# The second query group of an attention-and-MoE kernel in tiles of 128, 64 and 128 rows, the tile of 64 shared by two heads

## The chip, the cores and the metric

The kernel runs on one core of one Trainium2 chip. The metric is the device time of one execution in microseconds; smaller is better. TensorE (PE) multiplies and transposes into the accumulator banks, VectorE (DVE), ScalarE (ACT) and GpSimd (POOL) work on elements, SyncE (SP) issues the transfers.

## What is computed

Four batches of 576 positions and eight heads of 64 go through causal attention with a bias from a running sum, then 2304 rows of width 512 through two gated layers of hidden width 1536. Cut to what matters:

```
scores = scale * np.matmul(q, k.transpose(0, 1, 3, 2))
cum = np.cumsum(np.maximum(s, 0.0), axis=-1)
bias = -(cum[:, :, :, None] - cum[:, :, None, :])
scores = np.where(causal, -1e9, scores + np.minimum(bias, 0.0))
attn = softmax(scores)
x = np.matmul(attn, v)               # then 2304 rows of 512
xn = x / rms(x) * rms_g
x = (silu(xn @ w_gate) * (xn @ w_val)) @ w_out
x = (silu(x @ w2_gate) * (x @ w2_val)) @ w2_out
```

## The kernel before

The program is not written in its final order. Each step is given to a planner (`Plan`, `op`) with its engine, an estimated cost, what it reads and writes, and a rank (`pri`). The planner goes through the steps in its own time and issues on each engine the ready step of the lowest rank. A step of PE that another engine released counts as ready 1500 ns later (`SLACK`), unless PE has nothing else; one that PE's own last step released counts as ready at once. The order so found is the program's, fixed per engine.

*Heads.* The queries of a head fall into group A (0 to 255) and group B (256 to 575). Tiles are in `QT`; B has tiles 2, 3 and 4 with 128, 128 and 64 rows. Batches 0 and 1 do group A in a short form at the start (`EarlyUnit`); everything else goes through `Head` and `Unit`, one head after the other (`attend`): 32 heads have a group B, 16 of them also a late group A. Operands are split into a high and a low part (`kHH`, `kLL`; `H`, `L`), so a product of two needs two matmuls for attention and three for the gated layers.

For one head and group B: `scores` (L624) multiplies each query tile with the keys up to its last row: 384 columns for tile 2, 512 for tile 3, twice 288 for tile 4, each for `kHH` and `kLL` (L636). POOL writes the mask of the diagonal block (L650), DVE adds bias and takes the least (L662), ACT takes the exponential (L673). `values` (L678) transposes twelve blocks of 128x128 on PE into banks `tp` (L700), five, five and two; ACT copies each bank to `pTB` high (L705), DVE subtracts for `pTB` low (L708); ten value products (L716) of 320, 320, 320, 192 and 64 columns, high and low, sum the head's output. `pTB` is one pair of buffers for all heads. ACT and DVE carry the result to `x`.

*Gated layer.* When all eight heads of a group are done, `normalise` scales its rows and `moe1` multiplies them with the first weights (L929, 24 matmuls of 256 or 320 columns for each of 12 rows). These MoE products rank behind all heads (`P_MOE`), so PE takes them whenever no step of a head is ready. Behind the heads come the rest of these products, then the first output product in a Strassen form (L1281), the second layer (L1451, L1527) and the last output product (L1281, L1336).

*Start.* `setup` clears buffers on DVE and POOL: in `clear` the pads of `sq` and `qst`, in `clear_scores` all of `sc4` outside its own rows (L536, L537), as a tile of 64 rows is transposed with 128.

## Time and profile before

| what | value |
|---|---|
| median of three runs | 1064.9 us (1063.16 to 1066.07) |
| the profiled execution | 1063.1 us, of which the traced span 1061.3 us |
| PE busy | 1045.8 us, 99% |
| DVE, ACT, POOL busy | 784.7, 640.6, 222.2 us |
| granted TensorE clock | 1.0 throughout, the level of 2.4 GHz |
| moved by DMA | 206.97 MB, mean 195 GB/s |

Busy time is the union of the instructions' rows. A matmul's row lasts until its result has drained, and the next starts inside it, so PE can be busy all the time and still have matmuls further apart than their columns ask for; the timeline's starts tell the distance. A window's row gives each engine's busy time in a stretch. The chain of waits follows the program back from its end.

### The profile page before, as it was taken

What the parts mean: (1) busy time and instruction counts of PE and PEld (TensorE: products, weight loads), DVE (VectorE), ACT (ScalarE), POOL (GpSimd) and SP (SyncE); (2) the same over time, 40 slices, a digit from 0 to 9 for tenths busy, and PEclk for the clock granted to TensorE, in tenths of its full rate; (3) what the DMA queues carried; (4) which work ended last, traced back from release to release, by engine and by line L of the source; (5) the groups of instructions that cost most, each with busy time, mean ns of one, the idle gap of its engine ahead of it and who ended that gap; (6) DMA issues with size and microseconds to landing.
All of it is one profiled execution on the core that took longest, in us unless ns stands there. A gap on an engine that the chain in (4) does not pass through costs nothing.

```text
span 1061.3 us, 19650 instructions
## 1 busy us (share of the span) xinstructions
PE 1045.8 (99%) x6436; PEld 946.4 (89%) x6436; DVE 784.7 (74%) x1945; ACT 640.6 (60%) x1371; POOL 222.2 (21%) x302
## 2 busy tenths in 40 slices
PE   7999999999999999999999999999999999999998
PEld 5699999999999999999987889888888888878888
DVE  7898887877788876657779888566568766876462
ACT  6898767767664664333466766554556544664552
POOL 3157434423322420000000000222113220300000
PEclk9999999999999999999999999999999999999999
DMA  6785454333436652657588672675757667878773
GB/s 194 245 301 162 121 137 134 109 98 112 130 105 229 233 160 57 204 176 233 189 283 267 195 234 62 224 231 191 252 193 254 232 224 272 283 252 264 216 237 107
DMA packets 124822, 206.97 MB, mean 195 GB/s; under 512 B 15600, under 2 KB 52464, under 8 KB 124720
## 3 DMA queue, kind: packets, MB, share of 16 engines
q1 hardware_dynamic: 124672, 205.65, 61.1%
q8 instruction: 51, 0.84, 0.3%
q14 instruction: 51, 0.42, 0.1%
q10 hardware_dynamic: 48, 0.07, 0.0%
HBM read 141.09 MB, written 64.56 MB: 194 GB/s over the span
## 4 chain that ended last, share of the span: by engine, by line
PE 86%; DVE 2%; DMA 2%; ACT 1%; issue 1%; ACTq 0%; DVEq 0%; SPq 0%
PE mo L929 23%; PE mo L1451 10%; PE sps L1451 8%; PE mo L1281 8%; PE tp L1281 6%; PE sps L1281 5%; PE tp L700 4%; PE tp L716 4%; PE sps L636 4%; PE mo L1527 3%; PE sps L929 2%; PE tp L929 2%; PE mo L1336 2%; PE tp L1451 1%; PE mo L836 1%; DMA hh<-row0T 1%
## 5 line engine op out<-in xcount | busy, mean ns | idle before, releaser
L929 PE MATMUL mo<-xH,H 128*128 128x256 f32 (+1 forms) x672 | 200.4, 299 | 0.1
L929 PE MATMUL mo<-xH,L 128*128 128x256 f32 (+1 forms) x672 | 199.2, 297 | 0.0
L929 PE MATMUL mo<-xL,H 128*128 128x256 f32 (+1 forms) x672 | 199.2, 296 | 0.0
L1177 DVE TENSOR_TENSOR hL<-hh,hH 128x512 fp32r<-128x512 f32 (+1 forms) x192 | 125.7, 667 | 69.9 <-ACT hH L1174 69.2
L1174 ACT ACTIVATE hH<-hh 128x512 fp32r<-128x512 f32 (+1 forms) x192 | 114.7, 602 | 93.9 <-DVE hL L1177 20.8
L673 ACT ACTIVATE sc<-sc,col 128x512 f32<-128x512 f32 (+4 forms) x160 | 96.0, 601 | 52.6 <-DVE col L662 51.8
L929 PEld LDWEIGHTS mo<-xH,H 128*128 128x128 f32 x672 | 126.2, 188 | 1.0 <-issue 0.3
L929 PEld LDWEIGHTS mo<-xL,H 128*128 128x128 f32 x672 | 126.2, 188 | 0.9 <-issue 0.2
L929 PEld LDWEIGHTS mo<-xH,L 128*128 128x128 f32 x672 | 126.2, 188 | 0.4
L1281 PE MATMUL mo<-hH,wo 128*128 128x512 f32 x312 | 97.7, 389 | 0.0
L1281 PEld LDWEIGHTS mo<-hH,wo 128*128 128x128 f32 x312 | 58.6, 188 | 12.3 <-ACT hH L1174 0.2
L700 PE MATMUL tp<-ident,sc 128*128 128x128 f32 x432 | 66.5, 276 | 0.0
L936 ACT ACTIVATE t<-mo 128x256 f32<-128x256 f32 (+1 forms) x84 | 34.0, 405 | 52.3 <-PE mo L929 52.0
L708 DVE TENSOR_TENSOR pTB<-tp,pTB 128x512 fp32r<-128x512 f32 (+1 forms) x96 | 54.7, 575 | 9.6 <-ACT pTB L705 8.5
L1281 PE MATMUL mo<-hL,wo 128*128 128x512 f32 x156 | 61.0, 391 | 0.4 <-DVE hL L1177 0.4
L1281 PE MATMUL tp<-hH,wo 128*128 128x512 f32 x192 | 60.4, 389 | 0.0
L1457 ACT ACTIVATE u<-sps 128x512 f32<-128x512 f32 x48 | 28.5, 594 | 52.1 <-PE sps L1451 50.2
L705 ACT ACTIVATE pTB<-tp 128x512 fp32r<-128x512 f32 (+1 forms) x96 | 47.2, 501 | 13.6 <-PE tp L700 10.3
L938 DVE SCALAR_TENSOR_TENSOR t<-t,mo 128x256 f32<-128x256 f32 (+1 forms) x84 | 37.7, 449 | 23.3 <-ACT t L936 22.6
L636 PE MATMUL sps<-kHH,qst 128*128 128x288 f32 (+4 forms) x160 | 54.3, 348 | 0.1
L650 POOL TENSOR_SCALAR_AFFINE_SELECT sc<-cb 128x128 f32<-128x128 f32 (+1 forms) x128 | 41.2, 349 | 60.7 <-PE tp L700 26.7
L1281 PE MATMUL sps<-hH,wo 128*128 128x512 f32 x168 | 53.1, 390 | 0.7 <-ACT hH L1174 0.7
(253 smaller groups left out, 2807.8 us busy)
## 6 DMA issues: line engine op xcount, KB each, us to landing
raw<-in_w_gv SPq DMA_DIRECT2D x44, 511.8 KB, 5.1
tb<-h_d SPq DMA_DIRECT2D x48, 256.0 KB, 3.7
t<-tb SPq DMA_DIRECT2D x48, 256.0 KB, 2.4
hh<-t SPq DMA_DIRECT2D x48, 256.0 KB, 3.2
...
```

The source lines that it names most:

```text
L636: op(PE, c_mm(n), lambda en, pt=pt, o=o, c=c, n=n, z=z, kk=kk: en.matmul(pt()[:, :n], qst[j]()[:, o:o + 128], kk()[:, c:c + n], start=z == ...
L650: op(POOL, 165 + 0.85 * m, lambda en: en.affine_select(out=sc()[:m, o:o + m], in_=cb()[:m, o:o + m], pattern=[[-1, m]], base=0, compare_op ...
L673: op(ACT, c_act(o + m, 2) + 35, lambda en: en.activation(sc()[:m, :o + m], sc()[:m, :o + m], ACTF.Exp, scale=-1.0, bias=col()[:m, 0, t:t + 1],
L700: op(PE, C_TR, lambda en, pt=pt, a=a, m=m, kb=kb, t=t: en.transpose(pt()[:, a:a + P], self.sc[t]()[:, kb * P:kb * P + P], ident()), r=[sel ...
L705: op(ACT, c_act(n), lambda en, pt=pt, a=a, d0=d0, n=n, kn=kn: en.activation(H()[:kn, d0:d0 + n], pt()[:kn, a:a + n], ACTF.Copy), r=[pt], w ...
L708: op(DVE, c_tt(n), lambda en, pt=pt, a=a, d0=d0, n=n, kn=kn: en.tensor_tensor(out=L()[:kn, d0:d0 + n], in0=pt()[:kn, a:a + n], in1=f32(H() ...
L716: op(PE, c_mm(n), lambda en, w=w, z=z, kb=kb, d0=d0, n=n, o=o, kn=kn: en.matmul(po()[:, o:o + n], vst[j]()[:kn, kb, :], pT[g][z]()[:kn, d0 ...
L929: op(PE, c_mm(n), lambda en, a=a, x=x, c=c, k=k, i=i: en.matmul(ps()[:, :n], a()[:, c], x()[:, k, :n], start=(k == 0 and i == 0), stop=(k ...
L1174: op(ACT, c_act(n) + 35, lambda en: en.activation(H(), src(), ACTF.Copy), r=[src, *after], w=[H], pri=pri)
L1177: lambda en: en.tensor_tensor(out=L(), in0=src(), in1=f32(H()), op=ALU.subtract),
L1281: op(PE, c_mm(n), lambda en, m=m, w=w, xx=xx, kk=kk, i=i: en.matmul(ps[m]()[:, :n], w(), xx(), start=first and kk == 0 and i == 0, stop=kk ...
L1451: op(PE, c_mm(n), lambda en, w=w, xx=xx, cut=cut, kk=kk, i=i: en.matmul(ps()[:, :n], W[w]()[:, cut], xx(), start=first and kk == 0 and i == 0,
```

## The change

Tile 3 becomes 64 rows (384 to 447), tile 4 128 rows (448 to 575). The queries get 64 more columns (`QW`), zero at 448 to 511 for even heads and at 384 to 447 for odd ones, so that four matmuls, two of each head of a pair, sum both heads' tile 3 in one bank, 64 rows each (`PairTile.scores`, 448 columns). It has its own bias load (`cb3`), mask, least and exponential, once per pair. `turn` transposes its four blocks for both heads; the first head's part goes to `pTB`, the second's is parked, and `second` copies it into `pTB` by POOL or ACT between the two heads' value products. A head of its own keeps tiles 2 and 4: eight transpositions in two banks, and ten value products of 320, 320, 320, 192 and 128 columns, the first two of which read the pair's part. `sums` adds the pair's totals to the rows' at the end of a batch. `setup` clears less. The MoE products of batch 1, group B get ranks among the heads of batch 2.

```diff
-QT = [(0, 128), (128, 128), (256, 128), (384, 128), (512, 64)]
+QT = [(0, 128), (128, 128), (256, 128), (384, 64), (448, 128)]
+QCOL = (0, 128, 256, 384, 512)
+QW = 640
+CHUNKS = {"A": (0, 128), "B": (0, 128, 192)}
...
-    sq = [buf("m1", f"sq{i}", [P, 384], F32) for i in range(2)]
+    sq = [buf("m1", f"sq{i}", [P, (320, 384)[i]], F32) for i in range(2)]
+    tot3 = [buf("m1", f"tt{i}", [P, NH // 2], F32) for i in range(2)]
...
+    sc3 = [buf("at", f"sc3{i}", [P, 512], F32) for i in range(2)]
+    park = [buf("ex", f"ext{i}", [P, 256], F32R, "park") for i in range(2)]
...
+            en.memset(sq[1]()[:, 256:], 0.0)
...
-            for i in range(2):
-                en.memset(f32(qst[i]()[:, S:]), 0.0)
...
-                    en.memset(b()[:64, S:], 0.0)
-                    en.memset(b()[64:, :], 0.0)
-            op([(POOL, 1500), (DVE, 1500)], 0, clear_scores, r=["early 2"], w=sc4, pri=6.5)
+                    en.memset(b()[:, S:], 0.0)
+                for b in sc3:
+                    en.memset(b()[:, 448:], 0.0)
+            op([(POOL, 600), (DVE, 400)], 0, clear_scores, r=["early 2"], w=[*sc4, *sc3], pri=6.5)
...
+            op(SP, 4 * D * (QW - c0), lambda en: en.dma_start(
+                out=self.ql()[:D, S + c0:], in_=qk[b, h, :D, 0, c0:]),
...
+            tiles = [t for t in self.tiles if t != 3]
+            for t in tiles:
...
+            for t in tiles:
...
+                at = QCOL[t]
...
+                        op(PE, c_mm(n), lambda en, pt=pt, at=at, c=c, n=n, z=z, kk=kk: en.matmul(
+                            pt()[:, :n], qst[j]()[:, at:at + 128], kk()[:, c:c + n],
...
-                chunks = [
-                    ([(3, 3), (3, 4), (4, 4), (0, 2), (0, 3)], [(0, 64, 512, P)]),
-                    ([(0, 4), (1, 2), (1, 3), (1, 4), (2, 2)], [(0, 576, 512, P)]),
-                    ([(2, 3), (2, 4)], [(0, 1088, 192, P)]),
-                ]
-                wins = [(0, 320, 320, 0, P, (0, 1)), (1, 640, 320, 0, P, (1,)),
-                        (2, 960, 320, 0, P, (1, 2)), (3, 64, 192, 128, P, (0,)),
-                        (4, 256, 64, 256, P, (0,))]
+                chunks = [[(0, 2), (0, 4), (1, 2), (1, 4)], [(2, 2), (2, 4), (4, 4), (3, 4)]]
+                wins = [(0, 0, 320, 0, (0, 2)), (1, 320, 320, 0, (0, 2)), (2, 640, 320, 0, (1, 2)),
+                        (3, 1088, 192, 128, (1, 2)), (4, 960, 128, 192, (1,))]
...
+            def place(b, c):
+                if g == "A":
+                    return b()[:, :384].rearrange("p (k c) -> p k c", c=P)
+                a = b()[:, 640 * c:640 * c + 640]
+                return bass.AP(a.tensor, a.offset, [a.ap[0], [320, 2], [192, 2], [1, P]])
+            def source(pt, c):
+                a = pt()[:, :P * len(chunks[c])]
+                if g == "A":
+                    return a.rearrange("p (k c) -> p k c", c=P)
+                return a.rearrange("p (k t c) -> p k t c", t=2, c=P)
+            for c, blocks in enumerate(chunks):
...
+                n = P * len(blocks)
+                for a, (kb, t) in enumerate(blocks):
+                    op(PE, C_TR, lambda en, pt=pt, a=a, kb=kb, t=t: en.transpose(
+                        pt()[:, a * P:a * P + P], self.sc[t]()[:, kb * P:kb * P + P],
...
+                op(ACT, c_act(n), lambda en, pt=pt, c=c: en.activation(
+                    place(H, c), source(pt, c), ACTF.Copy), r=[pt], w=[(H, c)], pri=pri)
+                op(DVE, c_tt(n), lambda en, pt=pt, c=c: en.tensor_tensor(
+                    out=place(L, c), in0=source(pt, c), in1=f32(place(H, c)), op=ALU.subtract),
+                   r=[pt, (H, c)], w=[(L, c)], pri=pri)
...
+    class PairTile:
+        count = 0
+        def __init__(self, heads, tot):
+            i = PairTile.count
+            PairTile.count += 1
+            self.heads, self.tot, self.pair = heads, tot, heads[0].h // 2
+            self.sc = sc3[i % 2]
+            self.cb = buf("at", "cb3", [P, 448], F32)
+            self.col = cols[nunit[0] % 4]
+            nunit[0] += 1
+        def load(self, pri):
+            for z, hd in enumerate(self.heads):
+                i = hd.b * NH + hd.h
+                op(SP, 4 * 64 * 448, lambda en, z=z, i=i: en.dma_start(
+                    out=self.cb()[64 * z:64 * z + 64],
+                    in_=cum_d[i:i + 1, :448].to_broadcast([64, 448])),
+                   r=["cum_d"], w=[(self.cb, z)], pri=pri, later=2500)
+        def scores(self, pri):
+            sc, cb, col = self.sc, self.cb, self.col
+            for m, base in ((P, -64), (64, 0)):
+                op(POOL, 165 + 0.85 * 64, lambda en, m=m, base=base: en.affine_select(
+                    out=sc()[:m, 384:448], in_=cb()[:m, 384:448], pattern=[[-1, 64]], base=base,
+                    compare_op=ALU.is_ge, fill=MASKED / SCALE, channel_multiplier=1),
+                   r=[cb], w=[sc], pri=pri)
+            pt = ps_ring("sps", 2)
+            for z, hd in enumerate(self.heads):
+                for y, kk in enumerate((kHH[hd.j], kLL[hd.j])):
+                    op(PE, c_mm(448), lambda en, z=z, y=y, kk=kk, j=hd.j: en.matmul(
+                        pt()[:, :448], qst[j]()[:, 384:512], kk()[:, :448],
+                        start=z == 0 and y == 0, stop=z == 1 and y == 1), r=[qst[hd.j], kk], w=[pt], pri=pri)
+            for c, w, bias in ((0, 384, cb), (384, 64, sc)):
+                op(DVE, c_tt(w), lambda en, c=c, w=w, bias=bias: en.tensor_tensor_reduce(
+                    out=sc()[:, c:c + w], in0=pt()[:, c:c + w], in1=bias()[:, c:c + w],
+                    scale=-SCALE, scalar=col()[:, 1, 3:4] if c else 3.0e38, op0=ALU.add,
+                    op1=ALU.min, accum_out=col()[:, 0 if c else 1, 3:4]),
+                   r=[pt, bias], w=[sc, (col, 3)], pri=pri)
+            p = self.pair
+            op(ACT, c_act(448, 2) + 35, lambda en: en.activation(
+                sc()[:, :448], sc()[:, :448], ACTF.Exp, scale=-1.0, bias=col()[:, 0, 3:4],
+                accum_out=self.tot()[:, p:p + 1]),
+               r=[sc, (col, 3)], w=[sc, (self.tot, p)], pri=pri)
+        def turn(self, pri):
+            sc = self.sc
+            pt = ps_ring("tp", 2)
+            for kb in range(4):
+                op(PE, C_TR, lambda en, kb=kb: en.transpose(
+                    pt()[:, kb * P:kb * P + P], sc()[:, kb * P:kb * P + P], ident()),
+                   r=[sc, ident], w=[pt], pri=pri)
+            def source(z):
+                return pt().rearrange("p (k z c) -> p k z c", z=2, c=64)[:, :, z]
+            H, L = pT["B"]
+            for z, (h, l, view) in enumerate((((H, 2), (L, 2), self.place),
+                                              ((park[0], None), (park[1], None), self.parked))):
+                op(ACT, c_act(256), lambda en, z=z, h=h, view=view: en.activation(
+                    view(h[0]), source(z), ACTF.Copy), r=[pt], w=[h], pri=pri)
+                op(DVE, c_tt(256), lambda en, z=z, h=h, l=l, view=view: en.tensor_tensor(
+                    out=view(l[0]), in0=source(z), in1=f32(view(h[0])), op=ALU.subtract),
+                   r=[pt, h], w=[l], pri=pri)
+        def place(self, b):
+            return b().rearrange("p (k c) -> p k c", c=320)[:, :, 128:192]
+        def parked(self, b):
+            return b().rearrange("p (k c) -> p k c", c=64)
+        def second(self, pri):
+            for b, src in zip(pT["B"], park):
+                op([(POOL, c_pts(256)), (ACT, c_act(256) + 35)], 0, {
+                    POOL: lambda en, b=b, src=src: en.tensor_scalar(
+                        out=self.place(b), in0=f32(self.parked(src)), scalar1=1.0, scalar2=1.0,
+                        op0=ALU.mult, op1=ALU.mult),
+                    ACT: lambda en, b=b, src=src: en.activation(
+                        self.place(b), f32(self.parked(src)), ACTF.Copy)},
+                   r=[src], w=[(b, 2)], pri=pri)
+        def sums(self, tot, pri):
+            for z in range(2):
+                op(ACT, 100, lambda en, z=z: en.activation(
+                    tot()[:64, 1, z::2], self.tot()[64 * z:64 * z + 64, :], ACTF.Copy),
+                   r=[self.tot], w=[(tot, ("pairs", z))], pri=pri)
...
-        nt = -(-n // P)
+        at = CHUNKS[g]
+        nt = len(at)
...
+        for pair in range(NH // 2):
+            heads, last = [], []
+            for z in range(2):
+                h = 2 * pair + z
+                hd = Head(b, h, S, 0 if "A" in gs else 256)
+                heads.append(hd)
+                for g, x, tot in zip(gs, xs, tots):
+                    units.append(hd)
+                    pri = P_ATT + len(units) - 1
+                    if g == gs[0]:
+                        hd.load(pri - 1000)
+                        hd.prep_qk(pri - 0.5)
+                        hd.prep_v(pri - 0.4)
+                    u = Unit(hd, g, x, tot)
+                    if g == "A":
+                        u.scores(pri)
+                        u.values(pri + 0.4)
+                        continue
+                    last.append(u)
+                    if z:
+                        both = PairTile(heads, tot3[b % 2])
+                        both.load(pri - 1000)
+                        both.scores(pri - 0.1)
+                    u.scores(pri)
+            both.turn(pri + 0.1)
+            last[0].values(pri + 0.2)
+            both.second(pri + 0.3)
+            last[1].values(pri + 0.4)
+        both.sums(tots[-1], P_ATT + len(units))
...
-    moe1([(1, "B", 1)], W1, P_MOE + 120, -1.0e4)
+    moe1([(1, "B", 1)], W1, P_ATT + 36, -1.0e4)
...
-    qk = np.stack([inputs["q"], inputs["k"]], axis=2).transpose(0, 1, 4, 2, 3)
+    qk = np.zeros((NB, NH, D, 2, QW), inputs["q"].dtype)
+    qk[:, :, :, 1, :S] = inputs["k"].transpose(0, 1, 3, 2)
+    q = inputs["q"].transpose(0, 1, 3, 2)
+    for z in range(2):
+        cut = 448 - 64 * z
+        qk[:, z::2, :, 0, :cut] = q[:, z::2, :, :cut]
+        qk[:, z::2, :, 0, cut + 64:] = q[:, z::2, :, cut:]
```

PE, value products of one head in group B of batch 0. Before: all ten in a row, then the transpositions of the next (`tp`, `sps`, `mo` are banks, `vst` the values, `sc` the exponentials, `xH`, `xL` the rows and `H`, `L` the weights of the gated layer).

```order
L716 MATMUL tp_1581<-pTB_999,vst_815 128x320
L716 MATMUL tp_1581<-pTB_1017,vst_815 128x320
L716 MATMUL tp_1581<-pTB_999,vst_815 128x320
L716 MATMUL tp_1581<-pTB_1017,vst_815 128x320
L716 MATMUL tp_1581<-pTB_999,vst_815 128x320
L716 MATMUL tp_1581<-pTB_1017,vst_815 128x320
L716 MATMUL tp_1581<-pTB_999,vst_815 128x192
L716 MATMUL tp_1581<-pTB_1017,vst_815 128x192
L716 MATMUL tp_1581<-pTB_999,vst_815 128x64
L716 MATMUL tp_1581<-pTB_1017,vst_815 128x64
L700 MATMUL tp_1600<-ident,sc_1389 128x128
L700 MATMUL tp_1600<-ident,sc_279 128x128 x2
```

Now, at a head of batch 1 (batch 0's look alike): behind the second four transpositions come two scores and one MoE product, then five value products; the row after these is again an MoE product, and the other five stand eighteen MoE products later.

```order
L712 MATMUL tp_2641<-ident,sc_2417 128x128
L712 MATMUL tp_2641<-ident,sc_273 128x128 x3
L643 MATMUL sps_2651<-kHH_717,qst_734 128x288
L643 MATMUL sps_2651<-kLL_736,qst_734 128x288
L1026 MATMUL mo_2610<-xH_672,L_1528 128x256
L724 MATMUL tp_2662<-pTB_974,vst_745 128x320
L724 MATMUL tp_2662<-pTB_985,vst_745 128x320
L724 MATMUL tp_2662<-pTB_974,vst_745 128x320
L724 MATMUL tp_2662<-pTB_985,vst_745 128x320
L724 MATMUL tp_2662<-pTB_974,vst_745 128x320
L1026 MATMUL mo_2671<-xH_1384,H_1504 128x256
```

The ten in a row have become five and five, and the fifth is the first that reads the second bank of transpositions.

PE, scores of tile 3 in batch 0. Before, once for each head:

```order
L929 MATMUL mo_1539<-xH_1409,H_324 128x256
L929 MATMUL mo_1539<-xL_1346,H_324 128x256
L636 MATMUL sps_1564<-kHH_783,qst_138 128x512
L636 MATMUL sps_1564<-kLL_802,qst_138 128x512
L929 MATMUL mo_1539<-xH_1409,L_335 128x256
L929 MATMUL mo_1539<-xH_1409,H_324 128x256
```

Now, once for two heads, with tile 4's scores ahead:

```order
L643 MATMUL sps_1435<-kHH_717,qst_734 128x288
L643 MATMUL sps_1435<-kLL_736,qst_734 128x288
L768 MATMUL sps_1440<-kHH_717,qst_734 128x448
L768 MATMUL sps_1440<-kLL_736,qst_734 128x448
L768 MATMUL sps_1440<-kHH_775,qst_786 128x448
L768 MATMUL sps_1440<-kLL_798,qst_786 128x448
L1026 MATMUL mo_1417<-xL_1327,H_240 128x256
```

Two of 512 columns for each head have become four of 448 for a pair.

POOL, in batch 0 (`kLL` and `qst` low parts of keys and queries, `cb` the bias). Before:

```order
L918 TENSOR_TENSOR xL_1346<-x_121,xH_1409 128x256 x4
L602 TENSOR_TENSOR vst_746<-vl_1227,vst_746 128x5x64
L650 AFFINE_SELECT sc_1516<-cb_1386 128x128
L593 TENSOR_TENSOR kLL_737<-lq_1272,kHH_719 128x576
L650 AFFINE_SELECT sc_1546<-cb_1386 128x128
L650 AFFINE_SELECT sc_282<-cb_1386 64x64
```

Now:

```order
L1015 TENSOR_TENSOR xL_1327<-x_121,xH_1384 128x256
L811 TENSOR_SCALAR pTB_985<-park 128x4x64
L1015 TENSOR_TENSOR xL_1327<-x_121,xH_1384 128x256 x3
L607 TENSOR_TENSOR vst_745<-vl_1218,vst_745 128x5x64
L598 TENSOR_TENSOR kLL_736<-lq_1266,kHH_717 128x576
L657 AFFINE_SELECT sc_1493<-cb_1352 128x128
```

A copy from the parked half (L811) has come between the row subtractions.

## Rows read from the trace of the kernel before

**Rows 1.** The page: engines, the chain that ended last, transpositions (columns: busy, mean ns).
```profile
PE 1045.8 (99%) x6436; PEld 946.4 (89%) x6436; DVE 784.7 (74%) x1945; ACT 640.6 (60%) x1371; POOL 222.2 (21%) x302
...
PE 86%; DVE 2%; DMA 2%; ACT 1%; issue 1%; ACTq 0%; DVEq 0%; SPq 0%
...
L700 PE MATMUL tp<-ident,sc 128*128 128x128 f32 x432 | 66.5, 276 | 0.0
```

**Rows 2.** Windows: length, busy PE, PEld, DVE, ACT, POOL (count), clock, DMA share, GB/s.
```profile
0.00:54.00 54.00, 44.98 (x243) 32.72 (x243) 43.38 (x152) 40.93 (x120) 15.19 (x29) 1.00 0.73 222
54.00:100.00 46.00, 45.69 (x360) 44.25 (x361) 42.59 (x143) 40.96 (x96) 29.96 (x40) 1.00 0.76 243
100.00:425.00 325.00, 324.07 (x2486) 320.51 (x2485) 255.57 (x906) 217.11 (x553) 109.41 (x180) 1.00 0.45 135
425.00:527.50 102.50, 102.50 (x761) 102.16 (x760) 70.26 (x148) 38.08 (x74) 3.15 (x4) 1.00 0.63 202
527.50:660.00 132.50, 131.60 (x644) 110.95 (x643) 112.90 (x187) 88.77 (x159) 2.91 (x2) 1.00 0.67 212
...
915.00:946.50 31.50, 30.77 (x135) 24.48 (x135) 25.39 (x37) 20.87 (x38) 5.89 (x4) 1.00 0.89 300
```

**Rows 3.** Who PE waited for: us in total, times, longest.
```profile
PE sps L779 <- DMA lq<-in_qk: 3.8, 1, 3.8
```

**Rows 4.** Timeline of PE in the second group: start us, us, line, shape, count.
```profile
143.68 0.53 PE L716 MATMUL tp<-pTB,vst 128*128 128x192 f32 x4
144.04 0.76 PE L700 MATMUL tp<-ident,sc 128*128 128x128 f32 x5
...
147.08 0.71 PE L700 MATMUL tp<-ident,sc 128*128 128x128 f32 x5
147.54 0.42 PE L636 MATMUL sps<-kHH,qst 128*128 128x384 f32 x1
147.80 0.34 PE L636 MATMUL sps<-kLL,qst 128*128 128x384 f32 x1
147.97 0.28 PE L929 MATMUL mo<-xL,H 128*128 128x256 f32 x1
...
149.14 0.39 PE L636 MATMUL sps<-kLL,qst 128*128 128x512 f32 x1
149.36 0.28 PE L929 MATMUL mo<-xL,H 128*128 128x256 f32 x1
149.48 0.28 PE L929 MATMUL mo<-xH,L 128*128 128x256 f32 x1
```

**Rows 5.** Timeline of PE: MoE products, and value products of the first group.
```profile
200.00 0.31 PE L929 MATMUL mo<-xH,L 128*128 128x320 f32 x1
...
200.59 1.41 PE L716 MATMUL tp<-pTB,vst 128*128 128x320 f32 x10
...
236.27 0.57 PE L716 MATMUL tp<-pTA,vst 128*128 128x256 f32 x4
236.67 0.36 PE L929 MATMUL mo<-xH,H 128*128 128x320 f32 x1
```

**Rows 6.** Groups by shape: ACT and DVE (60 to 425 us), POOL (all): busy us, mean ns.
```profile
L705 ACT ACTIVATE pTB<-tp 128x512 fp32r<-128x512 f32 x64 | 37.7, 591 | 9.6 <-PE tp L700 6.3 <-PE tp L716 2.4
...
L708 DVE TENSOR_TENSOR pTB<-tp,pTB 128x512 fp32r<-128x512 f32 x64 | 43.9, 688 | 8.9 <-ACT pTB L705 7.7
...
L593 POOL TENSOR_TENSOR kLL<-lq,kHH 128x576 fp32r<-128x576 f32 x24 | 34.6, 1442 | 40.5 <-ACT kHH L586 40.5
...
L602 POOL TENSOR_TENSOR vst<-vl,vst 128x320 fp32r<-128x320 f32 x30 | 26.7, 890 | 78.0 <-ACT vst L600 64.6 <-PE sps L636 8.6 <-DMA tb<-h_d 4.5
...
L435 POOL TENSOR_SCALAR H<-raw 128x512 fp32r<-128x512 f32 x8 | 5.2, 654 | 30.0 <-DVE raw L429 20.6 <-DVE rc L874 4.1 <-DVE fac L884 3.6
```

**Rows 7.** Timeline of DVE in the first stage.
```profile
17.58 0.59 DVE L537 MEMSET sc<- 64x640 f32 x1 [0.17 <-issue]
```

77 lines of the change are left out of this document (22 added, 55 removed).

## The prediction

> **What bounds the kernel now.** I read the page first. TensorE is busy 1045.8 us of 1061.3, and the chain that ended last is 86% PE [rows 1]: each microsecond of PE work taken away could be a microsecond of time. But a busy PE is not a full one, since an instruction's row lasts until its results have drained. So the cost of a matmul is read from one start to the next in the timeline: four 320-column MoE products start 0.59 us apart in all, 0.147 each, though each row lasts 0.31 [rows 5].
>
> Then the stages. From 54 us to the end of the heads at 425 PE idles 1.2 us of 371, and none from 425 to 527.5 [rows 2]. VectorE is at 42.6 of 46 at its worst there and 255.6 of 325 later. What PE waits for longest is the very first load, 3.8 us [rows 3]. Before 54 us PE is idle 9.0 us, with DVE at 43.4 and ACT at 40.9 of 54: that stage is set by short chains and loads. So the heads' stage is limited by PE, because MoE products fill what the heads leave, and the fill lasts to 527. A shorter softmax on ACT or DVE buys nothing there; fewer columns on PE do.
>
> **The change, part by part.**
>
> *Transpositions.* Before, a head of the second group has 12; now eight of its own and four for two heads, so ten: 64 fewer over 32 heads. Five start at 147.08 and the next matmul at 147.54, 0.46 us; that matmul then holds PE 0.26 us, its like behind it 0.17, so the five cost 0.55, 0.11 each [rows 4]. 64 x 0.11 = **7.0 us** off.
>
> The row of the group says 276 ns mean for a transposition [rows 1]; starts, not durations, queue up here, so I take 0.11. The Trainium skill (TensorE: Matmul & The Clock Gate, Part 4: PE-mode transpose) gives about 275 ns for one in a kernel's context, which the duration agrees with and the distance between starts does not; by that figure the term would be 17.6 us and the sum 18.6.
>
> *Scores of tile 3.* Two matmuls of 512 columns per head become four of 448 per pair, so 64 before and 64 now. A 512 takes 0.22 (149.14 to 149.36), a 384 takes 0.17 [rows 4]: 0.0004 us a column, 64 columns are 0.025 us, 64 times **1.6 us** off. Tile 4 keeps 4 x 288 columns.
>
> *Value products.* The block of 64 queries becomes one of 128: 64 matmuls grow. No row has this group with 128 columns. Two of 192 and two of 64 take 0.36 us (143.68 to 144.04), 0.09 each [rows 4]; in the first group two of 256 and two of 128 take 0.40 (236.27 to 236.67), and less 0.24 for the 256s (an MoE product of 256 takes 0.12, 149.36 to 149.48) a 128 costs 0.08 [rows 4, 5]. Bounds: nothing, or 64 columns at 0.0004, 64 times 0.025 = 1.6 us. I take **0**: a 128 has its own row, and it is no dearer than a 64's share.
>
> A rule stands against this term: the Trainium skill (TensorE: Matmul & The Clock Gate, Back-to-back issue gap) gives about 60 cycles for 1 to 64 columns and 134 for 128, which would be an estimated 2.0 us more over 64 matmuls. The trace shows 0.09 and 0.08 us for the two, each with its weight load; by the rule the sum would be 6.0 us off instead of 8.0.
>
> *Work beside PE.* DVE loses half of a 384-column and a 128-column pass per head, ACT half of a 512-column exponential; ACT gets 64 more columns of queries, POOL or ACT two copies per pair, SP 32 loads of 112 KB more, at 45% DMA share [rows 2]. ACT and DVE now write their parts in pieces of 64 or 128 columns, which no row shows: as long as before, or up to twice. All lies under PE: 0, unless PE waits for it (next but one). The moved products of the second batch are the same number at another rank: 0; PE has MoE products to fill with either way, up to 527 us.
>
> *Start.* Two memsets of 64x640 (0.59 us each) stand on DVE at 17 to 19 us, among the chains PE waits for [rows 7]; four of 64 columns replace them, at a tenth of the width. Between 0 and 1.0 us off; I take 0.4, since DVE is only one of three things waited for there. The memsets taken from the very beginning precede a wait for the first load: 0.
>
> *New waits.* The order shows one: in ten of the 32 heads the ten value products break off behind the fifth. That fifth reads what ACT copies from the second bank of transpositions, and stands 1.0 to 1.9 us of PE work behind the last of them (the fence of the change: two scores, one MoE product, four value products). It needs the drain (0.28 less 0.11 [rows 1]) and the copy (591 ns [rows 6]), so 0.76 us and two signals, met if ACT is free. Queued behind it on PE is all else, MoE products too. Bounds: 0, or ten times a whole other copy in front, 5.9 us. I take **1.0**, 0.1 each, nearer the first: ACT works 217 of 325 us. Before, the like distances were 2.0 us and more.
>
> The chain between two heads is longer but covered: value products of head one, then two copies of the parked half (128x512 takes 654 ns on POOL [rows 6]; 128x256 then 0.33 to 0.65, about 0.9 for two), then head two's. The order has 2.7 to 4.9 us of other PE work there in all 16 pairs. The new bias load waits on SP for the previous pair's tile; behind it are the next heads' loads and the hidden rows' stores, both a ring of two ahead: 0.
>
> *Sum.* -7.0 - 1.6 - 0.4 + 1.0 = -8.0. The profiled run took 1063.1 us (span 1061.3 and 1.8 around it), so its like comes to 1055.1. It lies 1.8 us under the median of the three, so against 1064.9 the forecast is **1056.9 us**, -0.75%.
>
> **The rivals.**
>
> *Head two waits for its pair (the slower side).* One pair of buffers holds both heads' probabilities: head two's first products need the third part, whose copies wait for head one's last product. If POOL has a key subtraction (1442 ns) or a value subtraction (890 [rows 6]) in front, two copies at 0.9 and signals come to 2.0 to 2.6 us; the ACT and DVE copies of head two's own parts (2 x 591 + 688) take 2.1. Against 2.7 us of cover at the tightest and mostly 3.5 to 4.5, it decides only when both lie in a row, 3.9 to 4.7 us, and the loss begins at 0.5 us of wait per pair (8.0 over 16). With 0.9 at each of 16 pairs: 1064.9 - 9.0 + 14.4 = 1070. For it: one buffer pair, and those two subtractions are POOL's longest work in the heads. Against: POOL is busy 109 of 325 us. Chance 0.09, at 1070.
>
> *The gain is given back behind the heads.* Products and row sums behind 527 us fetch from memory; PE waits 0.9 us from 527.5 to 660 and 0.7 from 915, the latter at 89% DMA share [rows 2]. If loads, not PE, set these stretches, arriving 8 us earlier only lengthens waits: 1064. Against: the stretch ahead runs PE without a gap at 63% share, so loads come early too. Chance 0.05.
>
> *Waits at the breaks at their upper end.* 5.9 in place of 1.0, and 1.6 for the wider value products: -7.0 - 1.6 - 0.4 + 5.9 + 1.6 = -1.5, 1063.4. Chance 0.08.
>
> *A transposition's duration is its price.* 64 x 0.276 = 17.7 in place of 7.0: 1046.2. The starts in [rows 4] speak against it. Chance 0.02. The Trainium skill (TensorE: Matmul & The Clock Gate, Part 4: PE-mode transpose) has nearly the same figure for one transposition.
>
> **How the numbers follow.** The forecast has 0.76, the four rivals 0.09, 0.05, 0.08, 0.02. About 0.3% (3.2 us: 1061.7 to 1068.1) is what a measurement here tells from no change. Faster: 0.76 + 0.02 + 0.02 of the cases that give part back = 0.80. Same: the rest of these, 0.11, and 0.01 of the first rival: 0.12. Slower: 0.08. The range: downward the value of 1056.9 less the new waits (1.0), the rest of the start (0.6) and 1.8 for the spread of runs, 1053.5; upward to 1063.5, which takes in the third rival and leaves out those at 1064 and more, and 1046: 0.16, and a little of the forecast's own tails.
>
> **What would show it.** In the profile after: 368 rows of transpositions in the second and first groups together in place of 432, at the same distance between starts; score matmuls of 448 columns at 0.20; two 192s and two 128s in 0.36 us; PE idle from 54 to 425 under 2.5 us; the first Strassen product some 8 us earlier than at 527.5, and the distance from there to the end unchanged at 534. Waits of PE at the value products for ACT above 3 us in total would speak for the third rival, for POOL or for DVE's second half for the first. If the heads end earlier but the Strassen part grows, the second is right. A start of the MoE products that moves by more than 1 us would make my first stage wrong.

## The result: slower by 0.9%, and the profile after

The changed kernel took **1075.6 us** (median of 6 runs, 1071.2 to 1078.7) against 1065.0 (1061.3 to 1068.1) of the kernel before: a ratio of 1.0091, interval 1.0065 to 1.0116. I had forecast 1056.9 and a range up to 1063.5. The profiled run took 1078.1 us, its span 1076.3. It lies 2.5 us above its median, and the profiled run before 1.9 below its own, so the two traces differ by 15.0 us where the medians differ by 10.6.

From the page of the changed kernel (engines with busy us, share and instructions; the chain that ended last; the own transpositions and the pair's are two groups, the second from the list by shape), to be read against [rows 1]:

```profile
PE 1051.4 (98%) x6372; PEld 947.4 (88%) x6372; DVE 778.9 (72%) x1882; ACT 634.4 (59%) x1355; POOL 234.4 (22%) x322
...
PE 75%; DVE 10%; DMA 6%; ACT 4%; issue 3%; SPq 1%; POOL 0%; DVEq 0%; ACTq 0%; POOLq 0%
...
L712 PE MATMUL tp<-ident,sc 128*128 128x128 f32 x304 | 47.1, 274 | 0.2 <-DVE park L798 0.2
L787 PE MATMUL tp<-ident,sc 128*128 128x128 f32 x64 | 10.0, 273 | 0.0
```

The work went as planned: 304 + 64 = 368 transpositions, 64 matmuls fewer, VectorE and ScalarE 6 us less busy. But the chain, 86% PE before, is 75% PE now, with 10% VectorE and 6% DMA in it. The stages (length, busy time of PE, PEld, DVE, ACT, POOL, clock, DMA share, GB/s), to be read against [rows 2]:

```profile
0.00:54.00 54.00, 45.78 (x245) 33.82 (x246) 40.95 (x148) 39.61 (x114) 16.85 (x29) 0.97 0.71 216
54.00:100.00 46.00, 42.76 (x321) 41.23 (x320) 40.44 (x129) 38.16 (x89) 31.05 (x42) 0.96 0.76 238
100.00:425.00 325.00, 318.04 (x2392) 311.43 (x2391) 252.55 (x856) 214.07 (x542) 119.40 (x198) 0.99 0.49 147
425.00:539.60 114.60, 114.60 (x831) 114.13 (x830) 73.83 (x155) 40.39 (x80) 2.47 (x3) 0.99 0.59 188
```

PE idles 3.2 + 7.0 = 10.2 us between 54 and 425 us, where it had idled 1.2, and its granted clock falls below 1.0, where it had been 1.0 throughout. The first Strassen product starts at 539.6 instead of 527.4: 12.2 us later, not 8 earlier. From there to the end it is 536.7 us instead of 533.9. So, in these two traces, 12.2 us are lost ahead of the Strassen part and 2.8 behind it.

The largest single loss is near 330 us. First VectorE (start, us, instruction, in brackets the idle time ahead of it and what ended it), then PE:

```profile
330.17 0.69 DVE L1310 TENSOR_TENSOR tb<-tb 128x512 f32<-128x512 f32 x1 [0.96 <-DMA tb<-h_d]
...
333.66 1.42 DVE L1310 TENSOR_TENSOR tb<-tb 128x512 f32<-128x512 f32 x2 [2.22 <-DMA tb<-h_d]
335.00 0.48 DVE L1038 TENSOR_TENSOR hh<-t,mo 128x320 f32<-128x320 f32 x1
```
```profile
333.55 0.31 PE L1026 MATMUL mo<-xH,L 128*128 128x320 f32 x1
335.62 0.39 PE L1006 MATMUL mo<-xL,sel 128*128 128x320 f32 x1 [1.76 <-DVE hh L1038]
...
338.04 2.44 PE L1006 MATMUL mo<-xL,sel 128*128 128x320 f32 x7
...
343.67 0.43 PE L1026 MATMUL mo<-xL,H 128*128 128x256 f32 x1 [0.95 <-DVE xL L1015]
...
345.39 0.41 PE L1026 MATMUL mo<-xL,H 128*128 128x256 f32 x1
345.60 0.41 PE L1026 MATMUL mo<-xH,L 128*128 128x256 f32 x1
...
347.54 0.28 PE L1026 MATMUL mo<-xH,L 128*128 128x256 f32 x1
347.66 0.28 PE L1026 MATMUL mo<-xH,H 128*128 128x256 f32 x1
```

L1310 is a subtraction for the row sums that only the Strassen part needs, 200 us later; its operand is still on its way from memory. VectorE works in order, so it stands still for 2.22 us, and `hh` (L1038) waits behind it. PE waits for `hh`, because only then a bank is free for the row factors (L1006) of batch 2. Filler is short here: behind the first L1006 stand the last 15 products of 320 columns, up to 338.04; from there on come batch 2's, which need the factors, and PE waits for them again. Products of 256 columns start 0.21 us apart from 344.96 on and 0.12 again from 347.30: in between the granted clock is at half, the level of 1.2 GHz.

To see all of it I summed, from the starts of PE's matmuls, the time from each to the next, up to the first Strassen product, by kind. What PE waits counts to the matmul ahead of the wait, and what a matmul holds back the next one counts to the next. e4 and g1 are two of the mended kernels below:

| us from start to next start | before | after | e4 | g1 |
|---|---|---|---|---|
| transpositions (480, now 416, with the short early heads) | 50.0 | 40.6 | 42.3 | 43.1 |
| scores (320) | 55.8 | 51.8 | 51.8 | 52.3 |
| value products (448) | 59.4 | 67.1 | 64.1 | 64.0 |
| MoE products and row factors (2336) | 320.2 | 335.1 | 325.1 | 323.8 |
| early heads and running sum | 20.4 | 23.2 | 21.6 | 21.7 |
| squares, transposed factors | 17.8 | 17.9 | 17.7 | 17.5 |
| sum | 523.6 | 535.8 | 522.6 | 522.4 |

Transpositions and scores give 13.4 us; 7.7 go at the value products, 14.9 at the MoE products (their work is unchanged, so it is waiting, half clock and what a transposition holds back, see e10), 2.8 at early heads and running sum. These kinds take in the start, which the change hardly touches: the 48 transpositions of the short early heads have 9.6 us before, 7.1 after, 8.3 in e4 and 8.2 in g1, and the early heads' value products 12.7, 13.4, 12.7 and 12.7. The start as a whole is only 1.2 us longer: the MoE products begin at 50.0 instead of 48.8.

### The profile page after: what moved, and what is told of

Read it like the earlier page. It is cut to its first block, busy times and chain, and to the rows that moved or that the text cites. A ratio compares the mean times of both kernels' runs of the same rounds, so it can differ in the third digit from the quotient of the medians.

```text
span 1076.3 us, 19524 instructions
## 1 busy us (share of the span) xinstructions
PE 1051.4 (98%) x6372; PEld 947.4 (88%) x6372; DVE 778.9 (72%) x1882; ACT 634.4 (59%) x1355; POOL 234.4 (22%) x322
## 4 chain that ended last, share of the span: by engine, by line
PE 75%; DVE 10%; DMA 6%; ACT 4%; issue 3%; SPq 1%; POOL 0%; DVEq 0%; ACTq 0%; POOLq 0%
PE mo L1026 20%; PE mo L1565 9%; PE mo L1395 8%; PE sps L1565 7%; PE tp L724 4%; PE tp L1395 4%; PE sps L1395 4%; PE mo L1641 2%; PE tp L712 2%; PE sps L643 2%; PE sps L1026 2%; PE tp L1026 2%; PE mo L1450 2%; DMA raw<-in_w_gv 2%; DMA tb<-h_d 1%
## 5 line engine op out<-in xcount | busy, mean ns | idle before, releaser
L1026 PE MATMUL mo<-xL,H 128*128 128x256 f32 (+1 forms) x672 | 203.1, 302 | 1.1 <-DVE xL L1015 0.9
L1026 PE MATMUL mo<-xH,L 128*128 128x256 f32 (+1 forms) x672 | 202.2, 301 | 0.0
L1026 PEld LDWEIGHTS mo<-xL,H 128*128 128x128 f32 x672 | 128.5, 191 | 1.9 <-DVE xL L1015 1.2
L1026 PEld LDWEIGHTS mo<-xH,L 128*128 128x128 f32 x672 | 128.5, 191 | 0.1
L680 ACT ACTIVATE sc<-sc,col 128x128 f32<-128x128 f32 (+3 forms) x128 | 73.1, 572 | 58.3 <-DVE col L669 57.4
L1571 ACT ACTIVATE u<-sps 128x512 f32<-128x512 f32 x48 | 28.5, 594 | 51.7 <-PE sps L1565 49.8
L724 PE MATMUL tp<-pTB,vst 128*128 128x320 f32 (+2 forms) x320 | 52.4, 295 | 2.1 <-DVE pTB L717 1.4
L724 PEld LDWEIGHTS tp<-pTB,vst 128*128 128x128 f32 x320 | 46.5, 189 | 5.0 <-DVE pTB L717 3.7
L717 DVE TENSOR_TENSOR pTB<-tp,pTB 128x512 fp32r<-128x512 f32 x64 | 44.0, 688 | 8.6 <-ACT pTB L715 7.7
L1038 DVE TENSOR_TENSOR hh<-t,mo 128x256 f32<-128x256 f32 (+1 forms) x84 | 37.8, 450 | 14.7 <-PE mo L1026 13.3
L712 PE MATMUL tp<-ident,sc 128*128 128x128 f32 x304 | 47.1, 274 | 0.2 <-DVE park L798 0.2
```

The source lines that it names most:

```text
L680: op(ACT, c_act(o + m, 2) + 35, lambda en: en.activation(sc()[:m, :o + m], sc()[:m, :o + m], ACTF.Exp, scale=-1.0, bias=col()[:m, 0, t:t + 1],
L712: op(PE, C_TR, lambda en, pt=pt, a=a, kb=kb, t=t: en.transpose(pt()[:, a * P:a * P + P], self.sc[t]()[:, kb * P:kb * P + P], ident()), r=[ ...
L717: op(DVE, c_tt(n), lambda en, pt=pt, c=c: en.tensor_tensor(out=place(L, c), in0=source(pt, c), in1=f32(place(H, c)), op=ALU.subtract), r=[ ...
L724: op(PE, c_mm(n), lambda en, w=w, z=z, kb=kb, d0=d0, n=n, o=o: en.matmul(po()[:, o:o + n], vst[j]()[:, kb, :], pT[g][z]()[:, d0:d0 + n], s ...
L1026: op(PE, c_mm(n), lambda en, a=a, x=x, c=c, k=k, i=i: en.matmul(ps()[:, :n], a()[:, c], x()[:, k, :n], start=(k == 0 and i == 0), stop=(k ...
L1038: op(DVE, c_tt(n), lambda en: en.tensor_tensor(out=hh()[:, :n], in0=t()[:, :n], in1=vp_()[:, :n], op=ALU.mult), r=[vp_, t], w=[hh], pri=pri)
```

## The experiments

"Before" stands for the kernel before, run in the same set. "Excess" in the expectations is the distance from one matmul's start to the next, less what its columns take without a wait (0.147 us for 320, 0.12 for 256), summed over a window. Behind the expectations it is given for the MoE products alone. A loss "by its own set" is a kernel's median less that of the kernel before in the same set, 10.6 us for the changed kernel; the interval of that one is some 2.7 us to either side.

### The moved rank and the row sums' subtractions

Theory R: the rank of batch 1's products costs it. Theory D: VectorE's subtractions that wait for their loads. Theory T: the tiles themselves.

**e1_rank_back**, the changed kernel with the rank undone:

```diff
-    moe1([(1, "B", 1)], W1, P_ATT + 36, -1.0e4)
+    moe1([(1, "B", 1)], W1, P_MOE + 120, -1.0e4)
```

> The changed kernel with one line undone: the MoE products of batch 1, group B rank behind all heads again (P_MOE+120 in place of P_ATT+36). Theory R (the rank costs it: between 300 and 375 us the changed kernel's TensorE stands 9.8 us longer between matmuls than before, in the windows 300, 325 and 350): 1075.6 - 9.8 = 1066 us, and the first Strassen product at 530 instead of 539.6. Theory T (the tiles cost it: pair, parked copies, broken value products): about as the changed kernel, 1074 to 1077. If my sum of -8.0 was right for the tiles alone and the rank is all that went wrong: 1057.

1069.8 us, before 1064.5, ratio 1.0050 (1.0028 to 1.0071). 5.8 us come back (by its own set the loss falls from 10.6 to 5.3): less than R's 9.8, far more than T's none. But the stall is still there with the rank undone, and VectorE's wait and PE's are as long as in the changed kernel; only the excess from 325 to 350 us is smaller, 4.8 for 7.0. VectorE's timeline of e1, and PE's:

```profile
337.07 1.42 DVE L1310 TENSOR_TENSOR tb<-tb 128x512 f32<-128x512 f32 x2 [2.43 <-DMA tb<-h_d]
338.40 0.48 DVE L1038 TENSOR_TENSOR hh<-t,mo 128x320 f32<-128x320 f32 x1
```
```profile
338.94 0.41 PE L1026 MATMUL mo<-xH,H 128*128 128x320 f32 x1 [1.79 <-DVE hh L1038]
```

**e2_rank_alone**, the kernel before with the opposite edit (`P_ATT + 36`):

> The kernel before with only the rank moved (P_ATT+36 in place of P_MOE+120), tiles as before. Theory R: the same stall appears near 325 to 345 us, the time goes to 1065.0 + 9.8 = 1075, and the granted clock falls under 1.0 behind the stall. Theory T: no change, 1064 to 1066, clock 1.0.

1069.0, before 1064.5, ratio 1.0038 (1.0012 to 1.0064). The kernel with the moved rank is 4.5 us slower without any new tile, and the clock in 325 to 350 us is 0.93. VectorE's row near 330 us is the same wait, though PE's longest wait from 300 to 360 us is 0.6 us, for ScalarE:

```profile
332.04 0.69 DVE L1196 TENSOR_TENSOR tb<-tb 128x512 f32<-128x512 f32 x1 [2.06 <-DMA tb<-h_d]
```

**e3_tb_later**, the changed kernel; the planner reckons 4 us more for these loads. It reckons about 3.05 us otherwise; the chain of the changed kernel has one of 5.24 us at 328.33:

```profile
328.33 5.24 DMA tb<-h_d
```

```diff
-            done = 2300.0 + took - ns
+            done = 2300.0 + took - ns + slow
...
+SLOW_TB = 4000.0
...
-               r=[*h_rows(gi, f), *after], w=[t], pri=pri, later=2000)
+               r=[*h_rows(gi, f), *after], w=[t], pri=pri, later=2000,
+               slow=SLOW_TB if p == 0 else 0.0)
```

> The changed kernel; the planner is told that the loads of the row sums' blocks (tb from h_d, first pair of row blocks) take 4 us longer than it assumes, so that VectorE's subtractions of them stand later in its order. Theory D (VectorE, stopped for 0.96 and 2.22 us at these subtractions while they wait for their DMA, holds up the work that gives TensorE its banks): those two waits go, and with them 3.2 us of stall and the 1.7 us of half clock behind it: 1075.6 - 4.9 = 1070.7. Theory R without D (the buffers of batch 0's and batch 2's rows are handed over too late, whoever waits): under 1.5 us gained, 1074 or more.

1067.2, before 1064.5, ratio 1.0022 (1.0007 to 1.0036): 8.4 us come back (by its own set the loss falls to 2.7), more than the 4.9 that D reckoned with; no wait of VectorE for these loads is left between 300 and 360 us. D has the right place. It does not follow that the later loads are what mended it: the edit makes the planner sort anew, and f3 and f4 below, which leave rank and loads as they are, have no such wait there either.

**e4_rank_and_tb**, both:

> The changed kernel with both undone steps together: the rank back behind all heads and the row sums' loads told 4 us longer. Each alone took 5.8 and 8.4 us off 1075.6. If they mend two stalls: 1061.4. If both mend the same stall (TensorE without work between 325 and 350 us, where the changed kernel's excess of distance between matmuls over their columns is 7.5 us, the rank's 4.8, the later loads' 1.9, before's 1.1): 1067, about as the later loads alone.

1065.6, before 1064.1, ratio 1.0011 (0.9992 to 1.0030). The two are one stall: together 10.0 us (by its own set the loss falls to 1.5), not 14.2.

**e7_before_tb_later**, the control:

> The kernel before with the later loads of the row sums alone: a control for the run that gained 8.4 us. If the gain there was the mending of a stall that the change brought: no gain here, 1064 to 1066. If later loads help any order: under 1061.

1063.6, before 1064.1, ratio 0.9996 (0.9983 to 1.0009): the kernel before had nothing there to mend.

**f2_before_rank_tb**, the kernel before with the moved rank and the later loads:

> The kernel before with the rank moved (alone 1069.0 us against 1064.5) and the later loads of the row sums. If the rank harms only because VectorE's subtractions then stand, waiting for their loads, ahead of what TensorE needs: 1064 to 1065. If the rank harms by itself (batch 1's products taken out of the fill that is needed at the end of batch 2): 1068 to 1070.

1068.0, before 1064.3, ratio 1.0025 (1.0000 to 1.0050). On the old tiles the later loads do not mend what the rank brought: it came to 1069.0 without them, and no wait of VectorE for these loads is left between 300 and 360 us. So what this kernel still loses is not lost by the subtractions; whether the rank itself loses it can't be told from the scatter of orders, next.

### What a new order costs by itself

Any edit makes the planner sort anew. So its constants were changed in the last digit, with the work untouched.

**e8_before_resorted** (`C_TR = 111` for 110) and **e11_before_resorted2** (13.0 for 13.3 in a matmul's cost), on the kernel before:

> The kernel before, its planner told 111 ns for a transposition instead of 110: no work changes, but the order does (some 370 places on TensorE). What a new order costs by itself. Theory N (the order of before is a lucky one among many, and any new one brings stalls of some us): 1067 to 1071. If orders are alike: 1063 to 1066.

> The kernel before, its planner told 0.3 ns less for every matmul: again no work changes, only the order. A second sample of what a new order costs; the first (111 ns for a transposition) came to 1069.0 against 1064.1. Theory N (the order of before is a lucky one): 1066 to 1070 again. If the first was an accident: 1063 to 1066.

1069.0 against 1064.1, ratio 1.0034 (1.0013 to 1.0055), and 1065.2 against 1063.9, ratio 1.0022 (1.0003 to 1.0041). Both slower, for nothing. In e11 VectorE waits 0.98 us twice for the loads of theory D, at 344 and 353 us, and PE is busy 20.00 of the 20 us from 340 on: such a wait brings PE no idle time where PE's next steps don't stand behind it.

**f3_after_resorted** and **f4_after_resorted2**, the same two edits on the changed kernel:

> The changed kernel, its planner told 111 ns for a transposition instead of 110: same work, another order. Theory N (the change's 11 us are mainly a bad order that any re-sort would shift): 1065 to 1071. If the loss belongs to the change in any order: 1073 to 1078, with the stall near 325 to 345 us again.

> The changed kernel, its planner told 0.3 ns less for every matmul: a second re-sort. Theory N: 1065 to 1071. If the loss belongs to the change in any order: 1073 to 1078.

1069.3, ratio 1.0033 (1.0010 to 1.0055), and 1065.8, ratio 1.0015 (0.9987 to 1.0044), both with before at 1064.3. The changed kernel's own order, 1075.6, is the worst of its three; the kernel before's, 1064 to 1065, the best of its three. By their own sets f3 and f4 lose 5.0 and 1.5 us. So 6 to 9 of the 10.6 us belong neither to the tiles nor to the rank as such, which are both in f3 and f4, but to the order that they happened to get: the excess from 325 to 350 us is 7.0 us in the changed kernel, 3.6 in f3, 1.0 in f4 and 0.4 before. Theory N is right for the changed kernel. The closest pair is f4 and g1 (below), with the same constants: g1 has rank and loads mended, f4 has not, and they take 1065.8 and 1065.5. In that order neither costs anything that the runs show.

### Where the 8 us are

Even mended, the tiles bring nothing: 1065.6 in e4. So the terms of the sum were taken one by one.

**e10_before_fewer**: the kernel before in exactly its order, 60 transpositions left out, the two of the third bank in 30 heads. The copies of that bank read `pTB` in its place, which takes 0.02 us longer on VectorE and 0.03 on ScalarE, 0.6 and 0.9 us in all.

```diff
+                    skip = g == "B" and hd.n_th > 1 and c == 2
-                    op(PE, C_TR, lambda en, pt=pt, a=a, m=m, kb=kb, t=t: en.transpose(
+                    op(PE, C_TR, lambda en, pt=pt, a=a, m=m, kb=kb, t=t, skip=skip: None if skip else en.transpose(
...
+                        return f32(H()[:kn, 64:64 + n]) if old else pt()[:kn, a:a + n]
```

> The kernel before in exactly its order, without 60 of the transpositions (the third bank of two, in 30 heads; the copies behind it read older probabilities, so those heads' outputs are wrong). The main term of my sum by itself: 60 x 0.11 = 6.6 us less, 1057.6. By the rows' duration, 60 x 0.276: 1047.6. If stalls take the place of the work: 1062 to 1064.

1062.7, before 1063.9, ratio 0.9992 (0.9980 to 1.0004): 1.2 us by the medians, of 6.6, and by the interval not told from none. Two things show in the trace. The price of a transposition was right. Before, one pair with the two matmuls behind it; then e10, the matmul ahead of the gap and the one behind it:

```profile
99.09 0.38 PE L700 MATMUL tp<-ident,sc 128*128 128x128 f32 x2
99.22 0.36 PE L929 MATMUL mo<-xH,H 128*128 128x256 f32 x1
99.42 0.34 PE L636 MATMUL sps<-kHH,qst 128*128 128x384 f32 x1
```
```profile
100.09 0.28 PE L935 MATMUL mo<-xH,H 128*128 128x256 f32 x1
100.21 0.34 PE L637 MATMUL sps<-kHH,qst 128*128 128x384 f32 x1
```

The product of 256 behind the pair holds PE 0.20 us, its like without the pair 0.12; with the pair's own 0.13 that makes 0.21. By the starts on both sides of each gap the 30 pairs gave 6.4 us, 0.22 in the median: 0.11 for one transposition, as forecast. And PE waits more. Whom PE waited for between 54 and 527 us (us in total, times, longest), e10 first, then before:

```profile
PE mo L842 <- ACT sq L836: 1.6, 2, 0.9
PE tp L722 <- DVE x L731: 1.2, 1, 1.2
PE tp L722 <- DVE pTB L714: 0.7, 1, 0.7
PE sps L637 <- DVE col L663: 0.6, 2, 0.4
PE mo L915 <- DVE x L919: 0.5, 1, 0.5
PE mo L915 <- DVE t L944: 0.2, 1, 0.2
PE mo L908 <- DVE sq L904: 0.2, 1, 0.2
```
```profile
PE mo L836 <- ACT sq L830: 1.4, 2, 0.8
PE mo L909 <- DVE x L913: 0.4, 1, 0.4
PE mo L902 <- DVE sq L898: 0.2, 1, 0.2
```

5.0 us instead of 2.0, nearly all of the increase for VectorE. From the first MoE product to the first Strassen product e10 is 1.0 us shorter (477.5 for 478.5): of 6.4 us of PE work saved 5.4 are given back, 3.0 of them in these waits and the rest in slower starts, mostly beside them. PE arrives sooner and finds VectorE not ready; the copies' own longer time may be a small part of it. By the Trainium skill's figure for a transposition (TensorE: Matmul & The Clock Gate, Part 4: PE-mode transpose, about 275 ns) the 60 would have been 16.5 us, an estimate; the trace agrees with that figure as a duration (274 ns in the changed kernel) and not as a price.

**e5_wide_product**: the kernel before in its order, the products of 64 columns made 128.

```diff
+                    g0, wide, at = (d0 - 64, 128, o - 64) if n == 64 else (d0, n, o)
```

> The kernel before in exactly its order; the two value products of 64 columns of each of 32 heads take 128 columns instead (the 64 added columns are summed into the wrong rows of the output). What one such product costs, alone. My term was 0: 1065.0. By the distance between starts in the trace of the changed kernel (97 ns for 128 columns, 80 for 64): 64 x 0.017 = 1.1 us more, 1066.1. By the upper bound of the term 1.6 more. In the trace the distance from a 128 to the next start tells it, whatever the times say.

1065.0, before 1064.5, ratio 0.9989 (0.9964 to 1.0013): the runs can't tell. The starts can. The 128s stand 0.097 us ahead of the next matmul on average (6.20 us for 64), the 64s stood 0.081 (5.17), which looks like 64 x 0.016 = 1.0 us. But the next matmul gives it back. Before, the five transpositions behind the 64s take 0.52 us to the next start; in e5, behind the 128s, 0.49:

```profile
144.04 0.76 PE L700 MATMUL tp<-ident,sc 128*128 128x128 f32 x5
144.56 0.36 PE L929 MATMUL mo<-xH,H 128*128 128x256 f32 x1
```
```profile
144.64 0.73 PE L700 MATMUL tp<-ident,sc 128*128 128x128 f32 x5
145.13 0.36 PE L930 MATMUL mo<-xH,H 128*128 128x256 f32 x1
```

From the first product of 192 to the second matmul behind the last product the two kernels differ by 0.01 us over all 32 heads. So the term of 0 was right. The Trainium skill (TensorE: Matmul & The Clock Gate, Back-to-back issue gap) has a 128 dearer than a 64, as the starts alone show; the estimate from its figures, 2.0 us, is not in the sum.

**e6_joined** (on e3) and **e9_rank_tb_joined** (on e4): the ten value products kept together.

```diff
-                wins = [(0, 0, 320, 0, (0, 2)), (1, 320, 320, 0, (0, 2)), (2, 640, 320, 0, (1, 2)),
+                wins = [(0, 0, 320, 0, (0, 1, 2)), (1, 320, 320, 0, (0, 1, 2)), (2, 640, 320, 0, (1, 2)),
```

> The changed kernel with the later loads of the row sums (1067.2 us) and the ten value products kept together: the first four, too, are planned behind the second bank of transpositions, so they can't be issued five and five. Theory B (the breaks cost waits of TensorE between value products: 0.31 at 71.6, 1.0 at 77.8 and six more of 0.19 to 0.35 us, 2.9 in all, with a drop of the clock now and then): 1067.2 - 2.9 = 1064.3, and no distance over 0.3 us from one value product to the next. If the wait only moves ahead of the first product: 1067.

> The changed kernel with the rank back, the later loads of the row sums and the ten value products kept together. The run with the first two took 1065.6 us; in its trace TensorE stands 3.1 us longer than before behind value products of 320 columns and 0.9 us ahead of the first of them. Theory B (these waits belong to the breaks): 1065.6 - 4.0 = 1061.6. If the waits move to another place of the order: 1064 to 1067.

1067.4, before 1064.1, ratio 1.0036 (1.0019 to 1.0052), and 1067.4, before 1063.9, ratio 1.0043 (1.0029 to 1.0057): nothing gained, and e9 is 1.8 us above e4. The waits from one value product to the next did go, from 3.4 us in e4 to 0.3 in e9 (by the starts of 320-column products, less the columns' time). They came back elsewhere. Whom PE waited for, e4 and then e9:

```profile
PE tp L725 <- DVE pTB L718: 1.4, 3, 0.8
...
PE sps L644 <- DVE col L670: 1.2, 2, 0.8
```
```profile
PE mo L999 <- DVE t L1036: 3.4, 1, 3.4
...
PE sps L644 <- DVE col L670: 1.4, 2, 1.2
```

The wait for VectorE at the value products has become a wait for VectorE at the row factors' transposition. Theory B falls: the breaks were where the lateness showed, not its cause.

**f1_copies_on_act** (on e4): the parked copies on ScalarE alone.

```diff
-                op([(POOL, c_pts(256)), (ACT, c_act(256) + 35)], 0, {
...
+                op(ACT, c_act(256) + 35, {
```

> The changed kernel with rank and loads mended (1065.6 us), its parked copies on ScalarE alone instead of GpSimd or ScalarE. Between 50 and 125 us GpSimd is busy 52.6 of 71 us there (43.3 before), VectorE's operations last 6.4 us longer than their kind elsewhere (2.6 before), and TensorE's excess of distance is 10.4 us (7.4 before). Theory P (GpSimd's added copies stretch VectorE's work, and TensorE waits for it): VectorE's stretch falls to about 3, TensorE's excess by up to 3 us, 1062.6. If VectorE's lateness has another cause: 1065 to 1067.

1064.5, before 1064.3, ratio 0.9992 (0.9968 to 1.0015). PE's excess from 50 to 125 us did not fall (7.6 us for e4's 7.0), and VectorE's stretched work fell only from 6.4 to 4.9 us (counted as in the last section): theory P falls; the 1.1 us against e4 are within what orders scatter.

**e12_mended_resorted**, **g1_mended_resorted2** and **g2_joined_on_act**: further orders of the mended kernel (e9 with `C_TR = 111`; e4 with 13.0 for 13.3; f1 with the joined products).

> The changed kernel with rank, loads and joined products as in the run sent beside it, and its planner told 111 ns for a transposition instead of 110. No work changes. If the order by itself is worth some us in this kernel too, it differs from the run beside it by 2 to 6 us, either way; if the mended order is robust, by under 1.5 us.

> The changed kernel with rank and loads mended, its planner told 0.3 ns less for every matmul (this re-sort alone brought the changed kernel to 1065.8). If the tiles save 8 us that a good order shows: 1057 to 1060. If the work saved is given back in waits in any order (the breaks 3 us, the stage from 50 to 125 us 3 us, 64 wider products 1 us, behind the heads 1 to 2): 1062 to 1067.

> The changed kernel with rank and loads mended, the value products joined and the parked copies on ScalarE alone. Same question, another order. If a good order shows the saving: 1057 to 1060. If it is given back: 1062 to 1067, with under 0.5 us of waits between value products and 2 to 4 us more at scores and at the row factors' transposition.

1064.1 (before 1063.9), ratio 0.9999 (0.9986 to 1.0013); 1065.5 (1064.1), ratio 1.0015 (1.0001 to 1.0029); 1063.9 (1064.1), ratio 0.9985 (0.9965 to 1.0005). Six mended orders lie between 1063.9 and 1067.4. None shows the 8 us, and none is faster than the kernel before by more than its interval.

## Why the prediction was wrong

What failed is the step from "PE is the bound" to "each microsecond of PE work taken away could be a microsecond of time". e10 takes 6.4 us of PE work away in an unchanged order, and 5.4 of these come back, mostly where PE waits for VectorE; six mended orders of the changed kernel are no faster than before. And the sum had no term for what a new order costs: two steps that it put at 0 (the moved products, and what lies beside PE) became, in the order that came of them, an excess of 7.0 us between 325 and 350 us (0.4 before) and a loss of 10.6 us in all. By the steps of the prediction; the sums by kind are those of the table.

- **Transpositions, -7.0.** The size was right for PE: e10 has 0.11 for each. Without the early heads' 48 the kind falls by 6.4 us in e4 and by 5.5 in g1, not counting what the last of a row holds back. That it comes off the end was wrong: e10.
- **Scores, -1.6.** -4.0 in e4, -3.5 in g1. Behind anything but a transposition the median 512 took 0.230 us and the median 448 takes 0.203: 1.7 us for 64, the size forecast. The rest is waits, and that fewer of them stand behind a transposition (14 of the 512s, at 0.313, 5 of the 448s in e4, at 0.287).
- **Value products, 0.** Right, by e5.
- **Moved products, "the same number at another rank: 0".** The number is the same, but the rank gave the kernel another order, and for that the sum had no price. With the rank alone the kernel before is 4.5 us slower (e2), and without it the changed kernel 5.8 faster (e1); yet re-sorts that move nothing do as much (e8 +4.9, f3 -6.3), and f4 has the rank and is as fast as g1, which has not. So a price of the rank itself is not shown. How it can cost is argued, not shown: batch 1's products, taken out among the heads, are missing as a filler when batch 2's heads are done. There PE stands still for 1.76 and 0.95 us, but in e1, without the rank, for 1.79 too. I had named the end of the filler at 527 us and not the moments in between when one batch's products end and the next batch's wait for `normalise`.
- **Beside PE: 0, "unless PE waits for it".** PE waits for it. The row sums' subtractions, which I did not list as moved at all, stand in VectorE's order ahead of what frees PE's banks; planned later they give back up to 8.4 us together with a new order (e3). That the rank brought them there is not shown: in e1, without it, they stand there too.
- **New waits, 1.0.** 3.1 us at the 320-column products (0.3 before, 3.4 in e4), between the bounds of 0 and 5.9. The mechanism was off too: I had the fifth product wait for ScalarE's copy at ten breaks. At these products PE waits 1.4 us for VectorE in the changed kernel and 0.2 for ScalarE:

```profile
PE tp L724 <- DVE pTB L717: 1.4, 3, 0.8
...
PE tp L724 <- ACT pTB L715: 0.2, 1, 0.2
```

  The sixth product waits for VectorE's low part of the second bank, 0.69 us of work behind the copy that I had priced [rows 6]. The first head shows it: four of its products start at 72.2 to 72.7, the fifth at 77.70, and the sixth, with no break in the order ahead of it, waits for the low part.

```profile
77.70 0.31 PE L724 MATMUL tp<-pTB,vst 128*128 128x320 f32 x1
78.85 0.81 PE L724 MATMUL tp<-pTB,vst 128*128 128x320 f32 x5 [0.84 <-DVE pTB L717]
```

- **Start, -0.4.** Not seen. The MoE products start at 50.0 instead of 48.8, which I had put down as a sign against my first stage; but e5 and e10, with the start of before, have 49.4 and 49.8, so a microsecond there says nothing.
- **Behind the heads unchanged.** 533.9 us became 536.7, in e4 534.8, in g1 534.4. But kernels with the old tiles have 532.8 (e5) to 536.5 (e8) there, so nothing of it can be laid on the change or on the second rival.

Of the rivals, none was it. Head two does not wait for its parked half: PE's waits name none of these copies. The waits at the breaks were the right place with a price of 3, not 5.9, and the 1.6 for wider products that went with them is 0. The gain given back was the nearest, but I had it behind the heads and for loads, while it is given back among the heads and for VectorE.

The reasoning behind all of this was one reading: PE has no gap from 54 us on, so PE is the bound. [rows 2] has VectorE at 42.6 of 46 us in the same line, 93%, and at 79% after that; I read it as room. It is little room: e10 shows that in this order VectorE's results arrive just as PE comes for them, so that less PE work is mostly more PE waiting. The table has the same for e4's trace: 11.7 us saved at transpositions and scores (1.2 of it at the early heads, against the 1.2 that the rest of the start loses), 4.6 given back at value products (1.0 of it back again at the matmuls behind them, by e5), 4.9 at MoE products, and 0.9 behind the heads: 0.1 us in the end. By the medians e4 is 1.5 us slower than before, inside its interval.

Left open: how much of the 4.9 us at MoE products belongs to the tiles and how much to having any other order. Two re-sorts of the kernel before, with no new tile, cost 4.9 and 1.4 us themselves, and in their traces the MoE entry of the table rises by 2.8 and 1.6; to part the two would take many orders of each kernel.
